# A softplus feed-forward behind decay attention: blocks of 512 tokens in place of 256, and a planner that writes out every engine's order

## The chip, the cores and the metric

The kernel runs on one core of one Trainium2 chip. A core has five engines, each with its own queue of instructions: TensorE (PE in the profile; its weight loads are shown apart as PEld), VectorE (DVE), ScalarE (ACT), GpSimd (POOL) and SyncE (SP), which here only issues DMAs. They work side by side and wait for each other by semaphores. The metric is the device time of one execution in microseconds (us); lower is better.

## The reference

Attention with a decaying state per head, then a feed-forward layer with softplus:

```python
for t in range(S):                      # q, k, v: 4 batches, 8 heads, 768 tokens, 64 wide
    state = gamma[None, :, None, None] * state + np.einsum('bhd,bhe->bhde', k[:, :, t], v[:, :, t])
    y[:, :, t] = scale * np.einsum('bhd,bhde->bhe', q[:, :, t], state)
x = np.ascontiguousarray(y.transpose(0, 2, 1, 3)).reshape(B * S, H * D)      # 3072 tokens x 512
h = x @ w_in                            # 512 x 2048
g = np.maximum(h, 0.0) + np.log1p(np.exp(-np.abs(h)))
return (g @ w_out).astype(np.float32)   # 2048 x 512
```

The weights are float64 in memory; the kernel reads them as pairs of 32-bit words and makes float32 of them.

## The kernel before, in words

**Attention** is cut into 48 units: 4 batches, 6 chunks of 128 tokens, two halves of four heads. Inside a chunk it is matrix work: scores of the chunk (`sc`), masked below the diagonal; the state that the chunk adds (`pp`, kept as `td`); and the outputs (`yp`), scores times values plus queries times the state so far (`st`). A unit begins with transposes of k and q (`tp`), and its outputs go into `xh` and `xl`, the layer's input. The decay is in tables: GpSimd scales q and v (lines 120 and 121). A first chunk of a batch has no state to read, a last one none to make.

**Precision.** The large products are made of float32r matmuls on split operands: a value is a rounded part (`...h`) plus the rest (`...l`), and a product is three matmuls, hh, hl and lh (lines 289 to 291 and 319 to 321). The splitting is work for ScalarE (the rounding copy), VectorE or GpSimd (the subtraction). The first `WHOLE` = 8 units aren't split: their matmuls are float32 (lines 166, 194, 243 and 249), which take two instructions each and fewer on ScalarE and VectorE.

**The feed-forward** takes blocks of T = 256 tokens. A step is a pair of the 16 slices of 128 hidden columns: `hidden` has 24 matmuls of 256 columns into one PSUM bank `hp`; softplus is VectorE (line 296), ScalarE (297), VectorE (301), all in place in `sp`, then ScalarE rounds to `gh` (303) and GpSimd makes `gl` (305); `second` has 12 matmuls of 512 columns (two slices, two token tiles, three products) into the two accumulators of the block. `second` runs `LAG` = 2 steps behind `hidden`. Blocks 0 and 1 are taken in four turns (`TURNS`), since the weights are not all there yet: 0 has three steps, 1 has six, 0 the rest, 1 the rest. A turn that does not end its block leaves its accumulators in SBUF as `part` (line 327), which is added at the end (331).

**The weights** are converted once, slice by slice, in the first part of the run (lines 82 to 95): a scaling by ScalarE, two or three bit operations on VectorE, a rounding by ScalarE, a subtraction by GpSimd, for `win` and `wout` each. Loads run `FETCH` = 3 slices ahead.

**What sets the order.** The source calls the parts of the units by ticks (`PARTS`, `tick`), mixed with the steps; the tile framework then schedules the instructions by its own simulated timeline, and each engine runs its queue in that order. PSUM has eight banks: two `hp`, two accumulators, one for the weights' bits (`wp`), three for attention. `sp`, `gh` and `gl` have two buffers each, k, q and v three.

Of the kernel before, what the change touches and what calls it, by code (L numbers as in the profile page):

```python
# [10 lines left out]
F32 = mybir.dt.float32  # L11
# [6 lines left out]
P = 128  # L18
C = 128
T = 256  # L20
AHEAD = 2
EARLY = 4
WHOLE = 8
TURNS = ((0, 0, 3), (1, 0, 6), (0, 3, 8), (1, 6, 8))
SPREAD = 8
LAG = 2
FETCH = 3
SLACK = 2.0**-17


@with_exitstack
def decay_attention_then_softplus_ffn(ctx: ExitStack, tc: tile.TileContext, q, k, v, w_in, w_out, qtab, vtab, gtab, out):
# [6 lines left out]
    NP = NF // 2  # L39
    HH = H // 2  # L40
    NJ = HH // 2
    NT = T // P

    const = ctx.enter_context(tc.tile_pool(name="const", bufs=1))
    attn = ctx.enter_context(tc.tile_pool(name="attn", bufs=1))
    ffn = ctx.enter_context(tc.tile_pool(name="ffn", bufs=2))
    ps_h = ctx.enter_context(tc.tile_pool(name="ps_h", bufs=2, space=bass.MemoryType.PSUM))
    ps_o = ctx.enter_context(tc.tile_pool(name="ps_o", bufs=1, space=bass.MemoryType.PSUM))
    ps_w = ctx.enter_context(tc.tile_pool(name="ps_w", bufs=1, space=bass.MemoryType.PSUM))
    ps_a = ctx.enter_context(tc.tile_pool(name="ps_a", bufs=3, space=bass.MemoryType.PSUM))  # L50
# [3 lines left out]
    gtab_sb = const.tile([P, 2, H], F32, name="gtab_sb")  # L54
    qtabs = const.tile([P, NC, H], F32, name="qtabs")
    vtabs = const.tile([P, NC, H], F32, name="vtabs")
    ident = const.tile([P, P], F32, name="ident")


    raw, win, wout, converts = {}, {}, {}, {}  # L60

    def load_weights(f):
        fs = slice(f * P, (f + 1) * P)
        raw[f] = [const.tile([P, ND * P], I64, name=nm, tag=f"{nm}{f}") for nm in ("win", "wout")]
        loads_of_f = (
            nc.sync.dma_start(raw[f][0].rearrange("p (c w) -> p c w", c=ND), w_in[:, fs].rearrange("(c p) w -> p c w", p=P)),
            nc.sync.dma_start(raw[f][1], w_out[fs, :]),
        )

        if f >= FETCH:  # L70
            for load, after in zip(loads_of_f, converts[f - FETCH]):
                tc.add_manual_dep(load.ins, after.name, mybir.DependencyInfo(mybir.DependencyClass.Sync, mybir.DependencyReason.SCHED_ONLY), reason="pace")

    def convert_weights(f):

        n = ND * P
        converts[f] = []
        for nm, bits, to in zip(("win", "wout"), raw.pop(f), (win, wout)):
            words = bits.bitcast(U32).rearrange("p (n t) -> p n t", t=2)
            low, high = words[:, :, 0], words[:, :, 1]  # L80

            nc.scalar.activation(high.bitcast(F32), high.bitcast(F32), AF.Copy, scale=2.0**-112)

            wp = ps_w.tile([P, n], U32, name="wp")
            w = ffn.tile([P, n], U32, name="w", tag="o")

            if nm == "wout":
                nc.scalar.activation(wp, low, AF.Copy, scale=(1 - SLACK) * 2.0**-29, bias=7.5 * SLACK - 0.5)
            else:
                nc.vector.tensor_scalar(wp, low, 29, None, op0=ALU.logical_shift_right)  # L90
            nc.vector.scalar_tensor_tensor(wp, high, 0x80000000, wp, op0=ALU.bitwise_and, op1=ALU.bitwise_or)
            nc.vector.scalar_tensor_tensor(w, high, 3, wp, op0=ALU.logical_shift_left, op1=ALU.bitwise_or)
            to[f] = const.tile([P, 2, n], F32R, name=f"{nm}hl", tag=f"{nm}{f}")
            converts[f].append(nc.scalar.copy(to[f][:, 0], w.bitcast(F32)).ins)
            nc.gpsimd.tensor_tensor(to[f][:, 1], w.bitcast(F32), to[f][:, 0].bitcast(F32), op=ALU.subtract)
# [3 lines left out]
    loads, live, state, xs = {}, {}, {}, {}  # L99
    lo, up = slice(0, D), slice(D, P)  # L100


    kqs = [attn.tile([P, 3, 2, NJ, C], F32R, name=f"kq{i}") for i in range(2)]

    qws = [attn.tile([P, 2, NJ, C], F32, name="qw", tag="vhl", bufs=2) for i in range(2)]

    def load_unit(n):
        b, c, hf = units[n]
        tiles = []
        for nm, src in (("kn", k), ("qn", q), ("vn", v)):  # L110
            t = attn.tile([P, HH, D], F32, name=nm, bufs=3)
            nc.sync.dma_start(t, src[b, hf * HH:(hf + 1) * HH, c * C:(c + 1) * C, :].rearrange("h s d -> s h d"))
            tiles.append(t)
        loads[n] = tiles

    def decay(n):
        b, c, hf = units[n]
        kn, qn, vn = loads[n]
        hs = slice(hf * HH, (hf + 1) * HH)
        nc.gpsimd.tensor_tensor(qn, qn, qtabs[:, c, hs].unsqueeze(2).broadcast_to([P, HH, D]), op=ALU.mult)  # L120
        nc.gpsimd.tensor_tensor(vn, vn, vtabs[:, c, hs].unsqueeze(2).broadcast_to([P, HH, D]), op=ALU.mult)

# [324 lines left out]
```

## Time and profile before

| | |
|---|---|
| time, median of 3 runs | 703.34 us (702.11 to 703.37) |
| span of the profiled execution, first to last instruction | 700.0 us |
| its distance to that median, taken as what lies around the span | 3.34 us |
| mean granted clock of TensorE | 0.995 |
| TensorE busy | 682.3 us (97%) |
| VectorE, ScalarE, GpSimd busy | 453.1, 369.2, 284.1 us |
| DMA | 42.83 MB, 61 GB/s in the mean, 266 and 296 GB/s in the first two of 40 slices |

The runs give times alone, so the profiled execution is known by its span. In the page, slices are fortieths of the span (17.5 us). In a row of the timeline stand the start, the duration, engine, line, operation, output and inputs, shape and count, and in brackets how long the engine was idle before and what ended that. A matmul's duration holds its passage through the array and overlaps the next one; what a matmul costs in a row of them is the distance between starts. In a row of the groups stand the total, the mean in ns, and the idle time before.

### The profile page before, as it was taken

How to read it: one execution, taken by the hardware profiler on the slowest of the kernel's cores; microseconds unless marked ns; L12 is line 12 of the kernel's file. 1: busy time of each engine (PE TensorE's matmuls, PEld its weight loads, DVE VectorE, ACT ScalarE, POOL GpSimd, SP SyncE). 2: the span in 40 equal slices, each digit the busy share in tenths (PEclk: the TensorE clock that was granted, in tenths of full speed). 3: DMA queues.
4: the chain of work that ended last, by engine and by line, in shares of the span. 5: the costliest groups of instructions: out<-in, count | busy, mean ns of one | idle time of the engine just before them, and what ended most of it. 6: DMA issues, size and time to landing. Idle time of an engine off the chain costs nothing.

```text
span 700.0 us, 13586 instructions
## 1 busy us (share of the span) xinstructions
PE 682.3 (97%) x5056; PEld 621.6 (89%) x5056; DVE 453.1 (65%) x935; ACT 369.2 (53%) x831; POOL 284.1 (41%) x326
## 2 busy tenths in 40 slices
PE   5898999999999999999999999999999999999997
PEld 4687889999999999999999999999999999999996
DVE  5789979676666666567667766647766676544221
ACT  5888767555455545445555555545455545543221
POOL 6676566543343343344333333433442333222221
PEclk9999899999999999999999999999999999999999
DMA  9967452022112111111111111211211110000000
GB/s 266 296 188 188 120 173 59 16 61 68 32 23 69 24 32 58 36 31 54 39 24 31 53 38 24 61 31 31 62 25 38 54 31 16 31 1 1 31 1 30
DMA packets 90753, 42.83 MB, mean 61 GB/s; under 512 B 77376, under 2 KB 85568, under 8 KB 90688
## 3 DMA queue, kind: packets, MB, share of 16 engines
q1 hardware_dynamic: 90240, 41.96, 22.2%
q8 instruction: 40, 0.66, 0.4%
q14 instruction: 25, 0.20, 0.1%
q10 hardware_dynamic: 448, 0.01, 0.0%
HBM read 35.66 MB, written 6.29 MB: 60 GB/s over the span
## 4 chain that ended last, share of the span: by engine, by line
PE 93%; DVE 2%; ACT 1%; issue 1%; POOL 0%; ACTq 0%; DVEq 0%
PE hp L289 14%; PE hp L290 13%; PE hp L291 13%; PE acc L319 13%; PE acc L320 12%; PE acc L321 12%; PE sc L174 3%; PE pp L198 2%; PE tp L130 1%; PE yp L254 1%; PE yp L253 1%; PE tp L128 1%; PE yp L252 1%; PE yp L246 1%; PE yp L245 1%
## 5 line engine op out<-in xcount | busy, mean ns | idle before, releaser
L289 PE MATMUL hp<-xh,winhl 128*128 128x256 f32 x768 | 221.5, 289 | 1.2 <-DVE sp L301 1.1
L290 PE MATMUL hp<-xl,winhl 128*128 128x256 f32 x768 | 218.8, 285 | 0.0
L291 PE MATMUL hp<-xh,winhl 128*128 128x256 f32 x768 | 218.3, 284 | 0.0
L305 POOL TENSOR_TENSOR gl<-sp,gh 128x512 fp32r<-128x512 f32 x96 | 126.2, 1315 | 145.9 <-ACT gh L303 85.8
L319 PE MATMUL acc<-wouthl,gh 128*128 128x512 f32 x384 | 153.7, 400 | 0.0
L320 PE MATMUL acc<-wouthl,gh 128*128 128x512 f32 x384 | 150.5, 392 | 0.0
L289 PEld LDWEIGHTS hp<-xh,winhl 128*128 128x128 f32 x768 | 147.2, 192 | 3.1 <-issue 1.4
L321 PE MATMUL acc<-wouthl,gl 128*128 128x512 f32 x384 | 149.5, 391 | 0.0
L290 PEld LDWEIGHTS hp<-xl,winhl 128*128 128x128 f32 x768 | 148.0, 193 | 1.6 <-issue 0.3
L291 PEld LDWEIGHTS hp<-xh,winhl 128*128 128x128 f32 x768 | 147.8, 192 | 0.2
L296 DVE TENSOR_SCALAR sp<-hp 128x512 uint32<-128x512 uint32 x96 | 66.2, 690 | 69.7 <-PE hp L291 60.0
L303 ACT CAST gh<-sp 128x512 fp32r<-128x512 f32 x96 | 59.4, 620 | 76.4 <-PE acc L320 56.6
L120 POOL TENSOR_TENSOR qn<-qn,qtabs 128x256 f32<-128x256 f32 x48 | 29.7, 618 | 160.8 <-DMA qn<-in_q_dram 130.3
L297 ACT ACTIVATE sp<-sp 128x512 f32<-128x512 f32 x96 | 60.9, 634 | 53.2 <-DVE sp L296 52.8
L321 PEld LDWEIGHTS acc<-wouthl,gl 128*128 128x128 f32 x384 | 72.0, 188 | 15.7 <-issue 0.2
L319 PEld LDWEIGHTS acc<-wouthl,gh 128*128 128x128 f32 x384 | 72.4, 189 | 12.0
L320 PEld LDWEIGHTS acc<-wouthl,gh 128*128 128x128 f32 x384 | 72.5, 189 | 11.8 <-issue 0.2
L145 DVE TENSOR_TENSOR kq<-tp,kq 64x256 fp32r<-64x256 f32 x80 | 33.8, 422 | 68.9 <-ACT kq L143 67.5
L301 DVE SCALAR_TENSOR_TENSOR sp<-hp,sp 128x512 f32<-128x512 f32 x96 | 65.9, 687 | 13.0 <-ACT sp L297 11.7
L142 ACT CAST kq<-tp 64x512 fp32r<-64x512 f32 x80 | 46.5, 581 | 42.6 <-PE tp L130 41.6
L260 DVE TENSOR_TENSOR xl<-yp,xh 64x256 fp32r<-64x256 f32 x96 | 40.0, 417 | 32.0 <-ACT xh L258 30.9
L258 ACT CAST xh<-yp 64x256 fp32r<-64x256 f32 x96 | 35.1, 366 | 46.0 <-PE yp L254 43.6
(85 smaller groups left out, 1103.8 us busy)
## 6 DMA issues: line engine op xcount, KB each, us to landing
win<-in_moe_w_in_dram SPq DMA_DIRECT2D x16, 512.0 KB, 4.5
wout<-in_moe_w_out_dram SPq DMA_DIRECT2D x16, 512.0 KB, 4.0
kn<-in_k_dram SPq DMA_DIRECT2D x48, 128.0 KB, 2.3
qn<-in_q_dram SPq DMA_DIRECT2D x48, 128.0 KB, 2.8
vn<-in_v_dram SPq DMA_DIRECT2D x48, 128.0 KB, 2.2
out_dram<-o SPq DMA_DIRECT2D x24, 256.0 KB, 2.1
gtab_sb<-in_gtab_dram ACTq DMA_DIRECT2D x2, 2.0 KB, 3.9
qtabs<-in_qtab_dram ACTq DMA_DIRECT2D x1, 4.0 KB, 2.3
```

The source lines that it names most:

```text
L142: nc.scalar.copy(kq[own, :2, par], tp[own])
L289: nc.tensor.matmul(hp[:, k], lhsT=wt[:, 0, d, :], rhs=xh[:, d, :], start=d == 0, stop=False)
L290: nc.tensor.matmul(hp[:, k], lhsT=wt[:, 0, d, :], rhs=xl[:, d, :], start=False, stop=False)
L291: nc.tensor.matmul(hp[:, k], lhsT=wt[:, 1, d, :], rhs=xh[:, d, :], start=False, stop=d == ND - 1)
L296: nc.vector.tensor_scalar(sp.bitcast(U32), hps[s].bitcast(U32), 0x80000000, None, op0=ALU.bitwise_or)
L297: nc.scalar.activation(sp, sp, AF.Softplus)
L301: nc.vector.scalar_tensor_tensor(g, hps.pop(s), 0.0, g, op0=ALU.max, op1=ALU.add)
L303: nc.scalar.copy(gh, g)
L305: nc.gpsimd.tensor_tensor(gl, sps.pop(s), gh.bitcast(F32), op=ALU.subtract)
L319: nc.tensor.matmul(acc[i][t], lhsT=gh[:, k, ts], rhs=wt[:, 0], start=begins and k == 0, stop=False)
L320: nc.tensor.matmul(acc[i][t], lhsT=gh[:, k, ts], rhs=wt[:, 1], start=False, stop=False)
L321: nc.tensor.matmul(acc[i][t], lhsT=gl[:, k, ts], rhs=wt[:, 0], start=False, stop=ends and k == 1)
```

## The change

The file is written anew; the instructions of a unit, of a step and of a weight slice are as before, with these differences:

- **T = 512.** A feed-forward step is now one slice of hidden columns for 512 tokens: 12 matmuls of 512 columns into `hp`, the same chain of softplus, and 12 matmuls into four accumulators, all eight with gh first and then the four with gl (in the last step of a block token tile by token tile). There are 6 blocks of 16 steps. Only in block 0 four steps are made for half a block and two slices at a time, 256 columns wide, as soon as units 0 to 3 or 4 to 7 are there. No `part` is left.
- **WHOLE = 14**: units 8 to 13 are float32 too.
- **Banks and buffers.** Four accumulators, two `hp`, two banks `a0`, `a1` for attention and the weights' bits (early on the accumulators are lent to them). `sp` has one buffer in place of two; k, q and v have two in place of three, and three units at a time borrow the not yet loaded places of the last weights. `FETCH` is 2.
- **A planner.** All instructions are put in a list as operations with a cost, what they come after, the buffers they use and, for some, a due time. `Planner.order` plays that list with its costs and hand-over times, on each engine takes the operation that can start first and among those the one due first, and the instructions are then emitted in that order, each chained to the one before on its engine, so that the framework keeps it. The first three units' loads now stand ahead of the first weights in SP's queue.

The core of the diff:

```diff
-T = 256
-WHOLE = 8
-TURNS = ((0, 0, 3), (1, 0, 6), (0, 3, 8), (1, 6, 8))
-LAG = 2
-FETCH = 3
+T = 512
+W = 256
+WHOLE = 14
+BORROW = 8
+ORDER = ("u0", "u1", "u2", "u3", "u4", "h0", "u5", "h0", "u6", "u7", "h1", "h1")
+FETCH = 2
+HANDOVER = {
+    "PE": {"ACT": 210, "DVE": 250, "POOL": 300, "PE": 0, "SP": 300},
...
+                first = min(c[0] for c in starts)
+                if first >= 1e12 or best is not None and first >= best[0]:
+                    continue
+                s, b, op = min((c for c in starts if c[0] <= first + 1e-6), key=lambda c: (c[1] + COMFORT[e] > c[0], c[2].due, c[2].number))
...
+    hold_sp = holder(pool, [P, T], F32, "sp0")
+    hold_gh = holder(pool, [P, T], F32R, "gh0", "gh1")
+    hold_gl = holder(pool, [P, T], F32R, "gl0", "gl1")
...
-    def hidden(s):
-        i, p = steps[s]
-        xh, xl = xs[i]
-        hp = hps[s] = ps_h.tile([P, 2, T], F32, name="hp")
-        for k in range(2):
-            wt = win[2 * p + k].rearrange("p t (c f) -> p t c f", c=ND)
-            for d in range(ND):
-                nc.tensor.matmul(hp[:, k], lhsT=wt[:, 0, d, :], rhs=xh[:, d, :], start=d == 0, stop=False)
-                nc.tensor.matmul(hp[:, k], lhsT=wt[:, 0, d, :], rhs=xl[:, d, :], start=False, stop=False)
-                nc.tensor.matmul(hp[:, k], lhsT=wt[:, 1, d, :], rhs=xh[:, d, :], start=False, stop=d == ND - 1)
+    def ffn_step(s, h, i, f, when):
+        halves = slice(0, T // W) if h is None else h
+        n = 1 if h is None else T // W
+        width = T // n
...
+                    xh, xl = xt[:, 0, halves, d, :], xt[:, 1, halves, d, :]
+                    mm(o, wt[:, 0, d, :], xh, d == 0, False)
+                    mm(o, wt[:, 0, d, :], xl, False, False)
+                    mm(o, wt[:, 1, d, :], xh, False, d == ND - 1)
...
+        for part in range(1 if ends else 2):
+            for t in ts:
...
+                        if ends or part == 0:
+                            mm(bank(acc), buf(gh)[:, tt], wt[:, 0], begins and k_ == 0, False)
+                            mm(bank(acc), buf(gh)[:, tt], wt[:, 1], False, False)
+                        if ends or part == 1:
+                            mm(bank(acc), buf(gl)[:, tt], wt[:, 0], False, ends and k_ == n - 1)
```

How the order moves, at three places. First TensorE in the middle of the run, from a unit's transposes (`tp` before, L356 after) towards its scores (`sc` from `kq`). Before, the transposes:

```order
L289 MATMUL hp<-xh,winhl 128x256
L290 MATMUL hp<-xl,winhl 128x256
L291 MATMUL hp<-xh,winhl 128x256
L128 MATMUL tp<-ident,kn 128x128 x2
L130 MATMUL tp<-ident,qn 128x128 x2
L319 MATMUL acc_6363<-wouthl,gh 128x512
L320 MATMUL acc_6363<-wouthl,gh 128x512
L321 MATMUL acc_6363<-wouthl,gl 128x512
```

After, all of the way from the last transposes to the scores (`x` is the layer's input, `win` and `wout` the split weights, `a` a bank of attention):

```order
L356 MATMUL a_3767<-ident,qn_3478 128x128 x2
L270 MATMUL hp_3775<-x_68,win_933 128x512 x3
L270 MATMUL acc_3183<-wout_960,gh_3773 128x512 x2
L270 MATMUL acc_3190<-wout_960,gh_3773 128x512 x2
L270 MATMUL acc_3231<-wout_960,gh_3773 128x512 x2
L270 MATMUL acc_3213<-wout_960,gh_3773 128x512 x2
L270 MATMUL acc_3183<-wout_960,gl_3786 128x512
L270 MATMUL acc_3190<-wout_960,gl_3786 128x512
L270 MATMUL acc_3231<-wout_960,gl_3786 128x512
L270 MATMUL acc_3213<-wout_960,gl_3786 128x512
L270 MATMUL hp_3775<-x_68,win_933 128x512 x6
L270 MATMUL a_3813<-kq_67 128x256 x2
```

Hidden matmuls are 512 wide, the second product takes four accumulators, and 21 matmuls stand between a unit's transposes and its scores; before, behind the rows shown, it was a whole `second` (12), the outputs of the unit before (20 of 128 columns) and a whole `hidden` (24).

Second, TensorE near the end of the run. Before, the tail of the second product (`acc0`, `acc1`), where its last step's gh_8510 comes up for the first time:

```order
L319 MATMUL acc1_8288<-wouthl_1399,gh_8465 128x512
L320 MATMUL acc1_8288<-wouthl_1399,gh_8465 128x512
L321 MATMUL acc1_8288<-wouthl_1399,gl_8467 128x512
L319 MATMUL acc0_8287<-wouthl_1514,gh_8510 128x512
L320 MATMUL acc0_8287<-wouthl_1514,gh_8510 128x512
L319 MATMUL acc1_8288<-wouthl_1514,gh_8510 128x512
L320 MATMUL acc1_8288<-wouthl_1514,gh_8510 128x512
L321 MATMUL acc0_8287<-wouthl_1514,gl_8512 128x512
```

After, from the last hidden step to the same place (gh0_7114 and gl0_7118 come from the hidden step ahead, hp1_7050; gh1_7134 and gl1_7136 from the last one, hp0_7097):

```order
L270 MATMUL hp1_7050<-x1_69,win14_1310 128x512 x3
L270 MATMUL hp0_7097<-x1_69,win15_1363 128x512 x12
L270 MATMUL acc0_6639<-wout14_1457,gh0_7114 128x512 x2
L270 MATMUL acc1_6643<-wout14_1457,gh0_7114 128x512 x2
L270 MATMUL acc2_6675<-wout14_1457,gh0_7114 128x512 x2
L270 MATMUL acc3_6663<-wout14_1457,gh0_7114 128x512 x2
L270 MATMUL acc0_6639<-wout14_1457,gl0_7118 128x512
L270 MATMUL acc1_6643<-wout14_1457,gl0_7118 128x512
L270 MATMUL acc2_6675<-wout14_1457,gl0_7118 128x512
L270 MATMUL acc3_6663<-wout14_1457,gl0_7118 128x512
L270 MATMUL acc0_6639<-wout15_1486,gh1_7134 128x512 x2
L270 MATMUL acc0_6639<-wout15_1486,gl1_7136 128x512
```

Before, the last hidden matmul stands 24 matmuls of the second product ahead of the first one that reads gh_8510; after, 12 ahead of the first one that reads gh1_7134, and gl1_7136 is wanted two matmuls later.

Third, ScalarE in the start, at the first units behind the eighth, with weights (`raw`, `win`, `wout`, `w`) and softplus (`sp`, `gh`) around it. Before, unit 9 is split (`kq`, `vhl`, `ah` in two pieces):

```order
L142 CAST kq_82<-tp 64x2x256
L143 CAST kq_82<-tp 64x256
L142 CAST kq_82<-tp 64x2x256
L143 CAST kq_82<-tp 64x256
L82 ACTIVATE wout<-wout 128x512
L297 ACTIVATE sp<-sp 128x512
L149 CAST vhl<-vn 128x4x64
L94 CAST winhl<-w 128x512
L88 ACTIVATE wp<-wout 128x512
L303 CAST gh<-sp 128x512 x2
L176 CAST ah<-sc 128x256 x2
```

After, unit 8 is float32 (`kh` and `qw` are plain copies of the transposes):

```order
L473 CAST x_69<-a_1086 64x2x128
L372 COPY kh_1118<-a_1040 128x256
L374 COPY qw_73<-a_1040 64x256
L294 ACTIVATE raw<-raw 128x512
L473 CAST x_69<-a_1086 64x2x128
L294 ACTIVATE raw<-raw 128x512
L298 ACTIVATE a_1145<-raw 128x512
L317 CAST win_1152<-w_1143 128x512
L540 ACTIVATE sp_1150<-sp_1150 128x512
L317 CAST wout_1174<-w_1168 128x512
```

The four casts to `kq` and the one to `vhl` are gone; in their place stand two copies.

More of the change, by code (lines that the diff above doesn't have):

```diff
@@ new lines, with __init__ @@
+class Op:
+    def __init__(self, engine, cost, run, after, uses, at):
+        if engine in ("ACT", "DVE", "POOL"):
+            cost *= SLOW
+        self.engine, self.cost, self.run, self.uses, self.at = engine, cost, run, uses, at
+        self.after, self.then, self.start, self.end = [], [], None, None
+        for a in after:
+            if a is not None and a not in self.after:
+                self.after.append(a)
+                a.then.append(self)
+        for u in uses:
+            u.users.append(self)
@@ L31, in decay_attention_then_softplus_ffn @@
+MARGIN = 0
+SLOW = 1.02
+SHARED = ("hp0", "hp1", "acc0", "acc1", "acc2", "acc3", "a0", "a1")
+COMFORT = {"PE": 0, "ACT": 100, "DVE": 100, "POOL": 100, "SP": 0}
 @with_exitstack
@@ L52, in decay_attention_then_softplus_ffn @@
-    nc.scalar.preload_act_table_set("softplus")
[L54 to L72, printed above, removed]
+    NB = B * S // T
@@ new lines, in decay_attention_then_softplus_ffn, with hl, PE, ACT @@
+    weights = {}
+    LATE = [f"{nm}{f}" for f in (NF - 1, NF - 2) for nm in ("win", "wout")]
+    def hl(nm, f):
+        if (nm, f) not in weights:
+            weights[nm, f] = pool.tile([P, 2, ND * P], F32R, name=f"{nm}{f}")
+        return weights[nm, f]
+    bank = buf
+    def PE(n, run, after, uses=(), at=None):
+        return plan.add("PE", n, run, after, uses, at)
+    def ACT(n, run, after, uses=(), at=None):
+        return plan.add("ACT", n, run, after, uses, at)
+    def DVE(n, run, after, uses=(), at=None):
+        return plan.add("DVE", n, run, after, uses, at)
@@ L74, in convert_weights, with POOL, DMA @@
+    def POOL(n, run, after, uses=(), at=None):
+        return plan.add("POOL", n, run, after, uses, at)
+    def DMA(size, run, after=(), uses=(), at=None):
+        return plan.add("SP", size / 316.0, run, after, uses, at)
+    mm = lambda o, l, r, start, stop: emit(nc.tensor.matmul(o, lhsT=l, rhs=r, start=start, stop=stop))
+    wdone, pace = {}, []
     def convert_weights(f):
         n = ND * P
[L77 to L85, printed above, removed]
-            if nm == "wout":
-                nc.scalar.activation(wp, low, AF.Copy, scale=(1 - SLACK) * 2.0**-29, bias=7.5 * SLACK - 0.5)
-            else:
[L90 to L95, printed above, removed]
@@ L411, in decay_attention_then_softplus_ffn @@
-    for s, (i, p) in enumerate(steps):
-        convert_to(2 * p + 2)
-        stages(s, plan[s])
-        convert_to(EARLY + s + 1)
-    for s in range(len(steps), len(steps) + LAG):
-        stages(s, done)
+        for t in ts:
+            acc, done = accs.pop((i, t))
+            ob = hold_w(queue=False)
+            if t % 2:
+                o = ACT(scalar_time(DM), lambda acc=acc, ob=ob: emit(nc.scalar.copy(buf(ob), bank(acc))), [done[-1]], [acc, ob], when[1] + 3000)
+            else:
+                o = DVE(vector_time(DM), lambda acc=acc, ob=ob: emit(nc.vector.tensor_copy(buf(ob), bank(acc))), [done[-1]], [acc, ob], when[1] + 3000)
+            r = slice(i * T + t * P, i * T + (t + 1) * P)
+            DMA(4 * P * DM, lambda r=r, ob=ob: emit(nc.sync.dma_start(out[r, :], buf(ob))), [o], [ob], when[1] + 3000)
@@ L420 @@
+    ordered = plan.order()
+    for op in ordered:
+        op.run()
 def kernel(**inputs):
```

714 lines of the change are left out of this document (446 added, 268 removed).

## The prediction

> **What bounds the kernel now.** I read the page first: the busy shares, the slices, and the engines of the chain that ended last.
>
> ```profile
> span 700.0 us, 13586 instructions
> PE 682.3 (97%) x5056; PEld 621.6 (89%) x5056; DVE 453.1 (65%) x935; ACT 369.2 (53%) x831; POOL 284.1 (41%) x326
> PE   5898999999999999999999999999999999999997
> PE 93%; DVE 2%; ACT 1%; issue 1%; POOL 0%; ACTq 0%; DVEq 0%
> ```
>
> TensorE (PE) is the bound: 93% of the chain, and full from the fifth slice to the last but one. Only slices 1 to 5 (the first 88 us) and the last one hold idle time. But "busy" overlaps (ends are modelled), so a full digit does not say how much work is in it. For that I take the groups by form and then the timeline of one steady stretch, where the distance from one start to the next is the price of a matmul.
>
> ```profile
> L289 PE MATMUL hp<-xh,winhl 128*128 128x256 f32 x768 | 221.5, 289 | 1.2 <-DVE sp L301 1.1
> L319 PE MATMUL acc<-wouthl,gh 128*128 128x512 f32 x384 | 153.7, 400 | 0.0
> L166 PE MATMUL sc<-qw,kw 128*128 128x128 f32 x64 | 11.4, 312 | 2.5 <-ACT qw L135 1.7 <-DVE qw L136 0.7
> ```
> ```profile
> 500.86 0.22 PE L252 MATMUL yp<-ah,vhl 128*64 128x128 f32 x1
> ...
> 501.58 0.33 PE L289 MATMUL hp<-xh,winhl 128*128 128x256 f32 x1
> 501.75 0.28 PE L290 MATMUL hp<-xl,winhl 128*128 128x256 f32 x1
> ...
> 504.50 0.64 PE L174 MATMUL sc<-kq 128*128 128x256 f32 x4
> 504.99 0.40 PE L319 MATMUL acc<-wouthl,gh 128*128 128x512 f32 x1
> 505.22 0.40 PE L320 MATMUL acc<-wouthl,gh 128*128 128x512 f32 x1
> ...
> 507.73 0.22 PE L198 MATMUL pp<-vhl,kh 128*64 128x128 f32 x1
> ...
> 508.17 0.36 PE L289 MATMUL hp<-xh,winhl 128*128 128x256 f32 x1
> 508.37 0.28 PE L290 MATMUL hp<-xl,winhl 128*128 128x256 f32 x1
> ...
> 694.21 0.39 PE L319 MATMUL acc<-wouthl,gh 128*128 128x512 f32 x1
> ...
> 695.34 0.39 PE L321 MATMUL acc<-wouthl,gl 128*128 128x512 f32 x1
> ```
>
> From 501.75 to 504.50 stand the other 23 matmuls of a hidden step, 256 columns each: 0.1196 us apiece. From 505.22 to 507.73 stand 11 of 512 columns: 0.228; in the tail, from 694.21 to 695.34, five: 0.226; I take 0.227. A float32r unit costs 0.49 for its scores (504.50 to 504.99), 0.44 for its states (507.73 to 508.17) and 0.06 for each output matmul (12 of them from 500.86 to 501.58). The first hidden matmul behind a piece of attention takes 0.17 or 0.20 in place of 0.12 (501.58 and 508.17): taking 0.09 behind the transposes too, some 0.22 a unit, and the change keeps these seams.
>
> Now the whole: 2304 x 0.1196 = 276 (three lines of 768), 1152 x 0.227 = 262, 40 float32r units 93 (0.36 for the transposes of each included, by pairs like the one at 511.34 below), 8 float32 units 28 (their prices below): 658 us of matmuls in a span of 700. Of the other 42, 4.4 lie behind the last matmul, 48 x 0.22 = 10.6 are seams, and 27 are lost in the first 90 us. So the change can gain by fewer us of matmul, or by a faster start.
>
> **The change, term by term.** The sum is made against the span, 700.0, and its own 3.34 us up to the median of the three runs (703.34) are kept.
>
> *Wider hidden matmuls.* Before, 2304 of 256 columns; after, the order holds 1104 of 512 and 96 of 256 (the four half-block steps). A pair of 256 costs 0.239, one of 512 costs 0.227: 1104 x 0.012 = **-13.2**, all on PE's path. From the two prices a matmul has 0.012 us that do not depend on its columns. The Trainium skill ("TensorE: Matmul & The Clock Gate", section "Back-to-back issue gap") puts the gap between warm matmuls at N / 2.4 + 2.5 ns, hence 0.0025 us of fixed cost; by that, an estimate from that page, the term would be 1104 x 0.0025 = -2.8 and the sum below 702.1. The trace does not agree: 0.1196 stands where the page would have 0.109. I go by the rows.
>
> *Six more units in float32* (8 to 13). Their price from the early units:
>
> ```profile
> 56.40 0.38 PE L243 MATMUL yp<-qw,st 128*64 128x128 f32 x2
> ...
> 57.49 0.38 PE L249 MATMUL yp<-ah,vn 128*64 128x128 f32 x2
> ...
> 59.06 0.83 PE L166 MATMUL sc<-qw,kw 128*128 128x128 f32 x6
> 59.82 0.68 PE L194 MATMUL pp<-vn,kn 128*64 128x64 f32 x8
> 60.42 0.72 PE L321 MATMUL acc<-wouthl,gl 128*128 128x512 f32 x2
> ```
>
> Outputs: 10 matmuls from 56.40 to 57.49, 0.109 each; scores 0.127 each (six in 0.76), eight a unit (64 for 8 units); states 0.60. Against a float32r unit: scores 1.02 for 0.49, states 0.60 for 0.44, outputs 16 x 0.109 = 1.74 for 20 x 0.06 = 1.20 (in a first chunk, without state, 0.87 for 0.72). Units 8 and 9 cost 1.23 more each, 10 and 11 (a last chunk, no states) 1.07, 12 and 13 (a first chunk) 0.84: **+6.3** on PE.
>
> *The start.* What the six units buy: ScalarE issues 7 instructions for a float32 unit against 13, VectorE 4 against 16.
>
> ```profile
> 6.00:20.00 14.00, 10.60 (x65) 8.20 (x66) 11.63 (x29) 10.91 (x26) 7.40 (x9) 1.00 1.16 316
> 20.00:60.00 40.00, 38.38 (x284) 32.03 (x284) 32.78 (x58) 33.58 (x75) 29.18 (x33) 1.00 0.83 229
> ...
> 66.00:68.00 2.00, 0.64 (x6) 0.40 (x4) 1.82 (x4) 1.93 (x5) 0.61 (x1) 1.00 0.68 231
> ...
> 70.00:72.00 2.00, 1.40 (x11) 1.13 (x11) 1.92 (x5) 1.32 (x3) 0.43 (x1) 0.50 0.85 266
> ```
>
> The columns are PE, weight loads, VectorE, ScalarE, GpSimd, granted clock. At 66 to 68 PE works 0.64 of 2 us while VectorE and ScalarE are over 90% full with the conversions of weights and the first split units; then the clock is at 0.50. The new order has less of that work at this place, and none of it is new. How much of the 27 goes? The latest thing in the new start is ScalarE: ahead of gh_825 (softplus of the third step, first half-block of the second pair) stand 16 + 6 + 13 instructions on weights, 9 copies of 512, 36 of 256, 16 of 128 and 6 of the softplus.
>
> ```profile
> L82 ACT ACTIVATE win<-win 128x512 f32<-128x512 f32 x16 | 11.0, 685 | 3.1 <-DMA win<-in_moe_w_in_dram 2.9
> L94 ACT CAST winhl<-w 128x512 fp32r<-128x512 f32 x16 | 9.9, 619 | 3.3 <-DVE w L92 3.2
> L167 ACT COPY ah<-sc 128x512 f32<-128x512 f32 x8 | 4.7, 581 | 0.5 <-PE sc L166 0.4
> L258 ACT CAST xh<-yp 64x256 fp32r<-64x256 f32 x96 | 35.1, 366 | 46.0 <-PE yp L254 43.6 <-PE yp L249 1.3
> L217 ACT COPY st<-td 64x128 f32<-64x128 f32 x6 | 1.8, 295 | 0.1
> ```
>
> 16 x 0.685 + 25 x 0.619 + 9 x 0.581 + 36 x 0.366 + 16 x 0.295 = 49.6 us. PE has 47.9 us of matmuls ahead of the same place (40 transposes 3.5, 72 scores 9.1, 64 states 4.8, 112 outputs 12.2, 96 hidden of 256 columns 11.5, 30 of 512 6.8), and some 2 of seams. If ScalarE starts at 6 us and is as full as before between 6 and 60 (44.5 of 54, 82%), gh_825 comes at 66.5, so 16.6 us are lost by then, and about 1 more behind it, since ScalarE's next 12 us of work (at 90%, 13.3) stand against 12.2 of PE: 17.7 lost in place of 27, a gain of 9. At 95% full it comes at 58.2 and the gain is 17. If the waits only move, it is 0. I take **-9**, by the fullness that the row shows.
>
> *The end.* Before, 24 matmuls of the second product stand between the last hidden matmul and the first one that reads its gh; after, 12, with one sp buffer in place of two. The chain behind a hidden step:
>
> ```profile
> 687.26 0.28 PE L291 MATMUL hp<-xh,winhl 128*128 128x256 f32 x1
> ...
> 687.65 0.69 DVE L296 TENSOR_SCALAR sp<-hp 128x512 uint32<-128x512 uint32 x1 [3.54 <-PE hp L291]
> ...
> 689.04 0.69 DVE L301 SCALAR_TENSOR_TENSOR sp<-hp,sp 128x512 f32<-128x512 f32 x1 [0.70 <-ACT sp L297]
> 690.10 0.62 ACT L303 CAST gh<-sp 128x512 fp32r<-128x512 f32 x1 [1.09 <-PE acc L320]
> ...
> 690.85 1.29 POOL L305 TENSOR_TENSOR gl<-sp,gh 128x512 fp32r<-128x512 f32 x1 [4.33 <-ACT gh L303]
> ```
>
> The hidden step ends at 687.38 (0.12 behind 687.26), and VectorE begins 0.27 later. The cast could have begun at 689.76, when VectorE was done; it waited 0.34 for its buffer, which is free in the new order. Without that wait gh is there 3.05 and gl 4.45 us behind the hidden step's end. In the new order the last hidden step ends 2.72 (12 x 0.227) behind the one ahead of it, and its sp has to wait for that step's gl: VectorE begins 1.75 behind its end in place of 0.27, so its gh is there at 4.55 and its gl at 5.95. PE waits 0.35 for the gh of the step ahead, works 2.72 to 3.05, waits 1.5 for the last gh, does two matmuls and waits 0.95 for the last gl: **+2.8**.
>
> *In between.* A unit's scores wait for the chain from its transposes:
>
> ```profile
> 511.34 0.38 PE L130 MATMUL tp<-ident,qn 128*128 128x128 f32 x2
> ...
> 515.06 0.43 DVE L146 TENSOR_TENSOR kq<-tp,kq 64x256 fp32r<-64x256 f32 x1
> ...
> 518.45 0.64 PE L174 MATMUL sc<-kq 128*128 128x256 f32 x4
> ```
>
> From the end of the transposes (0.14 behind 511.34) to the last kq (515.49) are 4.0 us, and PE had 7.0 us of other work there (to 518.45). In the new order it has between 4.3 and 5.3 in most units (the place in the order shown above: 21 matmuls of 512, 4.8). That fits with 0.3 to 1.3 to spare; a softplus instruction that gets into it makes a small wait. Bounds 0 and 23 (below); I take **+1.5**, nearer the row that fits.
>
> The evictions of partial sums (4, by VectorE and ScalarE) go; those engines have slack from slice 6 on, so 0. With GpSimd, seams and the last output copies nothing changes.
>
> Sum: -13.2 + 6.3 - 9 + 2.8 + 1.5 = -11.6. Span 688.4, time **691.7**.
>
> **The rivals.**
>
> The start does not get better: its waits move to ScalarE's copies of the first units, which have to go through before any weights are converted (three units' loads now stand ahead of the first weights on SP's queue). For it: ScalarE is on PE's heels by my own sum. Against: the clock drop at 70 came from a stall of split units that are gone. Time: 691.7 + 9 = 700.7.
>
> Width saves nothing: a hidden matmul of 512 columns costs what two of 256 cost, 0.239, since it is its weight load or its moving operand that sets the pace. For it: no row shows a hidden matmul of that width. Against: the second product has weights of the same 128 x 128 and 512 columns, and costs 0.227. Without the 13.2 the time is 704.9, which is at the edge of what can be told (+0.2%). The page named above lies between, at 702.1 by the estimate there.
>
> The fixed order makes waits in every unit: one VectorE instruction of the softplus (0.69 in the row above) gets into each of the 34 float32r chains of 4.0 us. PE takes its instructions in order, so each such wait is lost: 34 x 0.69 = 23.5 in place of 1.5, time 713.7. It is slower from a mean wait of 0.39 us a unit on ((11.6 + 1.5) / 34). For it: 4.3 is little more than 4.0. Against: before, ScalarE and VectorE are idle a third of a steady stretch, and any us that PE loses at seams gives them room.
>
> That the change doesn't do what it says can be left out: the order shows 512 columns and 14 float32 units.
>
> **How the numbers follow.** Forecast 0.66, no better start 0.18, no gain by width 0.04 (counted as same), waits in every unit 0.12. A measurement of this kernel can tell about 0.2% (1.4 us) from no change. Faster: forecast and worse start, 0.84. Same: 0.04. Slower: 0.12. Low end: start at 17 and no waits, 691.7 - 8 - 1.5 = 682, taken as 683; high end 702, which takes in the case of no better start and the upper bounds of the start in the forecast. Outside lie the waits in every unit (0.12), no gain by width (0.04) and the forecast's far edges.
>
> **What would show it.** Right: hidden matmuls start 0.227 apart; the slices show PE full from about 60 us, no slice with the clock down after 20; the last 10 us show PE idle for some 3 us, waiting for GpSimd's gl. Wrong: scores or outputs that wait on VectorE or GpSimd by 10 us in all; a hidden matmul at 0.239; PE not full before 85 us.

## The result, and the profile after

The changed kernel takes 692.93 us in the median of four runs (691.09 to 695.19), the kernel before 702.73 in four runs beside them: a ratio of 0.9863, 95% interval 0.9835 to 0.9891. Forecast were 691.7 us. The profiled execution took 691.09 us with a span of 689.4, 10.6 less than the span before.

The page, in the lines that answer to those of before:

```profile
span 689.4 us, 11100 instructions
PE 671.6 (97%) x3952; PEld 561.8 (82%) x3952; DVE 413.3 (60%) x867; ACT 358.7 (52%) x799; POOL 276.8 (40%) x320
PE   6998999999999999999999999999999999999995
PEclk9999999999999999999999999999999999999999
```

TensorE is at 8 or 9 from the second slice to the last but one, and in this execution the clock stays up, where before it fell at 70 us. Two windows of the start (columns as before: PE, weight loads, VectorE, ScalarE, GpSimd, granted clock):

```profile
20.00:60.00 40.00, 38.02 (x300) 33.94 (x299) 30.09 (x55) 31.74 (x71) 27.82 (x33) 1.00 0.73 211
60.00:82.00 22.00, 20.41 (x103) 16.56 (x101) 19.25 (x32) 17.43 (x32) 15.10 (x13) 1.00 0.50 171
```

ScalarE is 79% full between 20 and 60 us, where it was 84%, and 22 us around the old stall miss 1.6 us of TensorE's work.

The timeline of TensorE in a steady stretch gives the price of the new matmul:

```profile
305.28 1.52 PE L270 MATMUL hp<-x,win 128*128 128x512 f32 x6
306.64 0.64 PE L270 MATMUL a<-kq 128*128 128x256 f32 x4
307.12 2.91 PE L270 MATMUL hp<-x,win 128*128 128x512 f32 x12
309.86 0.22 PE L270 MATMUL a<-vhl,kh 128*64 128x128 f32 x1
```

Six hidden matmuls of 512 columns take 1.36 us (305.28 to 306.64), 0.227 each; twelve take 2.74, 0.228 each. The main waits of TensorE in the whole run, from the list of waits (sum, number, longest):

```profile
PE a L356 <- POOL qn L348: 4.7, 1, 4.7
PE hp L270 <- DVE sp L541: 1.6, 1, 1.6
PE acc L270 <- ACT gh L542: 1.4, 2, 1.2
PE hp L270 <- DVE x L474: 1.0, 1, 1.0
...
PE acc L270 <- POOL gl L543: 0.7, 1, 0.7
PE a L270 <- DVE td L485: 0.6, 1, 0.6
```

The first stands ahead of the first matmul of all, those on sp and x in the first 65 us, those on gh and gl in the last fourteen. Only the 0.6 on td (at 293 us) lies in the steady part. The end, from the timeline:

```profile
675.82 1.30 POOL L543 TENSOR_TENSOR gl<-sp,gh 128x512 fp32r<-128x512 f32 x1 [5.34 <-ACT gh L542]
677.15 0.69 DVE L539 TENSOR_SCALAR sp<-hp 128x512 uint32<-128x512 uint32 x1 [2.17 <-POOL gl L543]
...
679.99 0.73 PE L270 MATMUL acc<-wout,gh 128*128 128x512 f32 x2 [1.21 <-ACT gh L542]
...
681.40 0.50 PE L270 MATMUL acc<-wout,gl 128*128 128x512 f32 x1 [0.67 <-POOL gl L543]
...
683.57 0.39 PE L270 MATMUL acc<-wout,gl 128*128 128x512 f32 x1
684.83 0.59 ACT L576 COPY w<-acc 128x512 f32<-128x512 f32 x1 [1.61 <-DMA out_dram<-w]
685.54 0.69 DVE L578 COPY w<-acc 128x512 f32<-128x512 f32 x1 [2.91 <-ACT w L576]
```

VectorE cannot begin the last softplus before GpSimd has read the one sp buffer (677.15), and TensorE waits 1.21 and 0.67 for what comes of it. Behind the last matmul (683.57, its end 0.23 later) the third and fourth output copies wait for the stores of the first two, since there are two w buffers for four outputs: 5.6 us from the last matmul to the end of the span, 4.4 before.

### The profile page after: what moved, and what is told of

It is laid out like the page before. It is cut to its first block, busy times and chain, and to the rows that moved or that the text cites. A ratio compares the mean times of both kernels' runs of the same rounds, so it can differ in the third digit from the quotient of the medians.

```text
span 689.4 us, 11100 instructions
## 1 busy us (share of the span) xinstructions
PE 671.6 (97%) x3952; PEld 561.8 (82%) x3952; DVE 413.3 (60%) x867; ACT 358.7 (52%) x799; POOL 276.8 (40%) x320
## 3 DMA queue, kind: packets, MB, share of 16 engines
q1 hardware_dynamic: 90240, 41.96, 22.2%
## 5 line engine op out<-in xcount | busy, mean ns | idle before, releaser
L270 PE MATMUL hp<-x,win 128*128 128x512 f32 (+1 forms) x1200 | 297.7, 388 | 2.6 <-DVE sp L541 1.6
L270 PEld LDWEIGHTS hp<-x,win 128*128 128x128 f32 x1200 | 213.4, 188 | 42.8 <-issue 2.9
L270 PE MATMUL acc<-wout,gh 128*128 128x512 f32 x768 | 202.3, 395 | 1.4 <-ACT gh L542 1.4
L270 PEld LDWEIGHTS acc<-wout,gh 128*128 128x128 f32 x768 | 139.4, 188 | 29.7 <-ACT gh L542 2.3
L270 PE MATMUL acc<-wout,gl 128*128 128x512 f32 x384 | 108.8, 391 | 0.7 <-POOL gl L543 0.7
L270 PEld LDWEIGHTS acc<-wout,gl 128*128 128x128 f32 x384 | 71.2, 188 | 15.7 <-POOL gl L543 1.1
L412 ACT CAST kq<-a 64x512 fp32r<-64x512 f32 x68 | 39.5, 581 | 22.9 <-PE a L356 17.2
L348 POOL TENSOR_TENSOR qn<-qn,qtabs 128x256 f32<-128x256 f32 x46 | 28.5, 620 | 47.3 <-DMA qn<-in_q_dram 42.6
L270 PE MATMUL a<-ah,vhl 128*64 128x128 f32 x272 | 40.8, 222 | 0.0
L474 DVE TENSOR_TENSOR x<-a,x 64x256 fp32r<-64x256 f32 x86 | 35.8, 416 | 8.4 <-ACT x L473 7.1
L270 PE MATMUL a<-kq,st 128*64 128x128 f32 x240 | 34.1, 223 | 0.0
```

The lines of the kernel that those rows point to most:

```text
L270: mm = lambda o, l, r, start, stop: emit(nc.tensor.matmul(o, lhsT=l, rhs=r, start=start, stop=stop))
L348: scaled = lambda t, tab: emit(nc.gpsimd.tensor_tensor(t, t, tab[:, c, hs].unsqueeze(2).broadcast_to([P, HH, D]), op=ALU.mult))
L412: ck.append(ACT(scalar_time(512), lambda par=par, own=own: emit(nc.scalar.copy(KQ[int(kq.slot[-1])][own, par, :2], tpv()[own])), [tk, tq], ...
L474: xl.append(DVE(vector_time(256), lambda par=par, r=r: emit(nc.vector.tensor_tensor(xo(1, r), ypv()[:, par], xo(0, r).bitcast(F32), op=ALU ...
```

## The experiments

Theories: the terms of the prediction's sum, each with the reason given there, against the rivals named with each experiment. The last column is the median against that of the changed kernel in the first row. Not all of the kernels ran on the same chip, but each had the kernel before beside it (medians 702.24 to 702.98); taken from the ratios, the last column moves by 0.6 us at most. With intervals of about 0.15% on each side, differences below 1.5 us can't be told by time alone, and are read from rows. An edit of the changed kernel also goes through the planner, which may answer it with another order.

| kernel | median us | ratio to the kernel before, interval | against the changed kernel |
|---|---|---|---|
| the changed kernel again | 691.99 | 0.9849 [0.9834, 0.9864] | |
| hidden matmuls of 256 columns | 705.98 | 1.0042 [1.0028, 1.0056] | +14.0 |
| WHOLE = 8 | 730.23 | 1.0379 [1.0351, 1.0406] | +38.2 |
| WHOLE = 12 | 692.14 | 0.9850 [0.9834, 0.9865] | +0.2 |
| the kernel before with WHOLE = 14 | 702.09 | 0.9996 [0.9986, 1.0005] | |
| ScalarE: six bits instructions twice | 695.23 | 0.9897 [0.9877, 0.9917] | +3.2 |
| two sp buffers in the last block | 695.85 | 0.9905 [0.9891, 0.9918] | +3.9 |
| own sp for the last step | 692.17 | 0.9844 [0.9826, 0.9863] | +0.2 |
| four output buffers | 692.25 | 0.9857 [0.9839, 0.9875] | +0.3 |
| work ahead of the first load | 691.14 | 0.9839 [0.9824, 0.9853] | -0.9 |
| the three edges together | 688.89 | 0.9806 [0.9789, 0.9824] | -3.1 |
| the edges, bits on VectorE | 688.04 | 0.9795 [0.9779, 0.9810] | -4.0 |

### The width

```diff
+                    if h is None:
+                        z = d // NJ
+                        o = bank(hp).rearrange("p (a w) -> p a w", w=W)[:, z]
+                        for c in (2 * d % ND, 2 * d % ND + 1):
+                            mm(o, wt[:, 0, c, :], xt[:, 0, z, c, :], c == 0, False)
...
+                        return
```

> The 92 full hidden steps made of matmuls of 256 columns (24 a step) in place of 512 (12), all else as in the changed kernel. Theory: a pair costs 0.239 against 0.227, 1104 pairs, so +13.2 us against the changed kernel (about 705). Rival 1, the rule of the Trainium skill (TensorE: Matmul & The Clock Gate, Back-to-back issue gap), a fixed cost of 2.5 ns: +2.8 us (about 695). Rival 2: width costs nothing, 0 us (692).

Measured +14.0 us. In this kernel's timeline 24 hidden matmuls of 256 columns stand in a row:

```profile
311.71 3.04 PE L270 MATMUL hp<-x,win 128*128 128x256 f32 x24
314.59 0.22 PE L270 MATMUL a<-vhl,kh 128*64 128x128 f32 x1
```

2.88 us, 0.120 each, 0.240 a pair against 0.227. The order is otherwise that of the changed kernel, but for a stretch at about 160 to 180 us; between 100 and 200 us TensorE waits 0.9 us in all, where the changed kernel does not wait. By the rows 1104 pairs cost 13 to 14 us more. So the width alone is worth what the prediction took, and the two rivals (+2.8 and 0) fall.

### What the six float32 units buy

```diff
-WHOLE = 14
+WHOLE = 8
```

> Units 8 to 13 split again (WHOLE = 8), all else as in the changed kernel. Theory: TensorE has 6.3 us less of matmuls, but the start loses again what it lost before (27 us against 19.4 after), so +7.6 - 6.3 = +1.3 us against the changed kernel (-2 to +4), with ScalarE over 80% full from 20 to 60 us and gh of the third step later than 62.6 us. Rival 1: the fixed order alone mended the start, and the six units are a loss: -6.3 us. Rival 2: split units make more of the latency chain than before since k, q and v have two buffers: +10 us and more.

Measured +38.2 us. Only rival 2 has the size, and it is right about the latency chain; its reason, two buffers for k, q and v, does not show: no wait of TensorE between 100 and 200 us is for their loads. Rival 1 is right about the start, which is not worse: TensorE is busy 20.58 of 22 us between 60 and 82 us here, 20.41 in the changed kernel. The loss is later. Three windows of this kernel, one of the changed kernel, and this kernel's two largest waits between 100 and 200 us:

```profile
60.00:82.00 22.00, 20.58 (x101) 16.73 (x100) 19.17 (x35) 15.39 (x28) 14.60 (x13) 1.00 0.47 156
130.00:148.00 18.00, 13.87 (x68) 11.17 (x67) 12.53 (x23) 10.10 (x21) 7.81 (x9) 0.81 0.16 45
148.00:190.00 42.00, 22.39 (x154) 18.56 (x153) 27.79 (x68) 20.70 (x55) 9.77 (x16) 0.62 0.22 57
```
```profile
148.00:190.00 42.00, 42.00 (x263) 34.73 (x262) 31.74 (x69) 23.82 (x56) 17.15 (x21) 1.00 0.20 54
```
```profile
PE a L270 <- DVE al L446: 11.9, 9, 2.2
PE a L270 <- DVE x L474: 5.2, 3, 2.4
```

and the timeline of TensorE at that place:

```profile
148.13 0.39 PE L270 MATMUL acc<-wout,gl 128*128 128x512 f32 x1
...
152.07 0.47 PE L270 MATMUL a<-kq 128*128 128x256 f32 x2 [2.35 <-DVE x L474]
154.14 0.47 PE L270 MATMUL a<-kq 128*128 128x256 f32 x2 [1.60 <-DVE al L446]
...
190.67 1.63 PE L270 MATMUL hp<-x,win 128*128 128x512 f32 x3
```

At 148.13 the last matmul of block 0's feed-forward is done, and the next feed-forward matmul starts at 190.67: block 1 needs the units 8 to 15, and they aren't there. In between TensorE has only attention, and sits through the chain of every unit (al, x, td, kq). No other engine is full: VectorE works 27.79 of 42 us, ScalarE 20.70. With the gaps the clock falls to 0.62, so that the matmuls that are there take longer too. In the changed kernel the same 42 us are full at clock 1.00. So the float32 units, whose chain is short, don't relieve the start: they let eight units get done while block 0 still has feed-forward work to cover them. The scores that wait for al or x in the rows above read neither of them (their input is kq): they wait for the attention bank that they will write. There are two such banks, where the kernel before had three; what a third would have saved here was not tried.

How near the edge is this cover?

```diff
-WHOLE = 14
+WHOLE = 12
```

> WHOLE = 12: units 12 and 13 split, 8 to 11 float32. Theory: the float32 units buy that block 0's feed-forward steps cover the chain of the units that block 1 needs; with four of six the cover is short by the last units only, so -1.7 us of matmuls and +2 to +10 us of waits between 130 and 190 us (WHOLE = 8 lost 33 us there). Rival 1: the cover is enough with four, -1.7 us. Rival 2: any split unit among these brings the clock down and most of the loss, +20 us or more.

Measured +0.2 us. The list of waits has one of 1.4 (transposes on x) and one of 0.2 (on al) between 100 and 200 us, and the changed kernel has none there: 1.6 us lost for 1.7 of matmuls saved. That is a little below the 2 to 10 us of waits that the theory gave, and rival 1 (-1.7) can't be told from it by time. At twelve the first waits show; the other 38 us lie between twelve and eight, where nothing was run.

The same question in the old order:

```diff
-WHOLE = 8
+WHOLE = 14
```

> The kernel before with WHOLE = 14 and nothing else changed. The prediction's reason: units 8 to 13 in split form are what stalls TensorE between 60 and 80 us; in float32 some 5 us of the 27 lost at the start come back and the matmuls cost 6.3 more, so +1.3 us against the kernel before (-1 to +3), and the slices at 60 to 80 us are full. Rival 1: the start does not depend on these units, +6.3 us. Rival 2: as in the changed kernel with WHOLE = 8, the split units cost far more than they save also in the old order, so -5 us or more.

Measured 702.09 against 702.43 for the kernel before: no difference that can be told. What the six units cost in matmuls (6.3 us, as worked out) comes back. Between 64 and 72 us, where before PE was idle a third of the time and the clock fell, all is full:

```profile
64.00:68.00 4.00, 4.00 (x35) 3.58 (x35) 2.71 (x5) 2.85 (x8) 2.34 (x3) 1.00 0.64 177
68.00:72.00 4.00, 4.00 (x37) 3.93 (x37) 3.88 (x8) 3.16 (x7) 2.53 (x4) 1.00 0.90 236
```

So the prediction's reason holds for the old order, where units 8 and 9 stood in the start among the conversions of weights. In the new order TensorE loses no more there with WHOLE = 8 than with 14, as the 20.58 of 22 us above show.

### Is ScalarE the pace of the start?

```diff
+                if f < 6:
+                    b = ACT(
...
+                        [b], [wp, raw],
+                    )
```

> For the first six weight slices ScalarE makes the bits of wout twice (six more instructions of 0.63 us, 3.8 us of ScalarE's time, ahead of the third step's gh). The prediction's theory: ScalarE sets the pace of the start at some 80% full, so its gh comes 3.8 to 4.8 us later and the time rises by as much. Rival: the start is set by the chains between engines, and ScalarE's gaps take the extra work in: 0 to +1 us.

Measured +3.2 us, near the theory by size. By place it fits less well: gh of the third step begins at 63.53 against 62.56 in the changed kernel, 1.0 later and not 3.8. TensorE works 36.20 us between 20 and 60 in place of 38.02; the rest is small waits on several engines. The planner also answers the six instructions with another order from about 27 us on: the ninth gh starts at 99.76 against 102.52 in the changed kernel, the 26th at 231.84 against 229.39. So the 3.2 us are not lost at one place, and the run does not tell ScalarE's pace from the price of the other order. From the other side, on top of the kernel with the three edges (below):

```diff
-            if nm == "wout":
+            if nm == "none":
                 b = ACT(
```

> The kernel with the three edits at the edges, and the bits of wout made by VectorE as those of win are: ScalarE has sixteen instructions of 0.63 us less, six of them ahead of the third step's gh, VectorE sixteen of 0.69 more. Theory (six more of these on ScalarE cost about 3 us): six fewer bring back about as much, -2 to -3.5 us against the kernel with the edges alone (688.9), so about 686. Rival: VectorE is as full as ScalarE between 20 and 60 us (30 of 40), so the work only changes engines: -0.5 to +2.

Measured 688.04 against 688.89: -0.9, between theory and rival, and the intervals overlap. The window of 20 to 60 us of this kernel:

```profile
20.00:60.00 40.00, 37.33 (x293) 33.21 (x291) 36.83 (x68) 30.22 (x67) 29.07 (x33) 1.00 0.73 218
```

VectorE is 92% full in place of 76% (30.26 of 40 without this edit), and PE works 37.33 us there, 38.21 in the kernel without this edit. That speaks for a pace that ScalarE does not set alone, and for VectorE as the next limit. It is argued, not shown, since here too the order is another one, from about 20 us on.

### The spread, and the slow first matmuls

> The changed kernel unaltered, so that the variants beside it have it on the same chip. Theory: 691 to 694 us, ratio to the kernel before 0.983 to 0.990, with runs that spread by about 4 us where those of the kernel before spread by 1.5. Rival: the spread of the first runs was chance and closes to 1.5 us.

691.99 us, 690.53 to 693.58. The runs spread by 3.1 us, but in nine runs the kernel before has nearly the same, 2.7: nothing shows that the changed kernel spreads more, but the spread itself stays. Two profiles of the same order (the changed kernel, and the one with four output buffers, whose order differs in its last lines alone) show one source. The changed kernel, then the other (the `f32 x6` and `f32 x8` rows are scores of the first units):

```profile
8.16 0.94 PE L270 MATMUL acc<-qw,kh 128*128 128x128 f32 x6 [0.15 <-DVE qw L375]
...
10.53 1.16 PE L270 MATMUL a<-qw,kh 128*128 128x128 f32 x8 [0.24 <-ACT kh L372]
```
```profile
8.02 1.65 PE L270 MATMUL acc<-qw,kh 128*128 128x128 f32 x6 [0.19 <-DVE qw L375]
...
11.80 1.95 PE L270 MATMUL a<-qw,kh 128*128 128x128 f32 x8
```

The same eight scores take 1.95 us in place of 1.16. In one execution the array gets fast at about 8 us, in the other at about 13.4, though the granted clock of the windows reads 1.00 in both. The lead lasts: the 26th gh starts at 229.4 in the one and 231.4 in the other. The Trainium skill ("TensorE: Matmul & The Clock Gate", section "What's actually happening") says that the array starts throttled and is released after a window of about 3.4 us of sustained work, and that the window runs free of the kernel. The traces agree that the array starts slow; they don't agree with the 500 ns by which the moment varies there, since it varies by some 5 us between executions of one order.

A second source shows in the profile of the run just above, the changed kernel again. Its array gets fast at about 8 us too, and yet its 26th gh starts at 231.28. It waits 2.46 us for a softplus where the first profile waits 1.59:

```profile
63.21 2.90 PE L270 MATMUL hp<-x,win 128*128 128x512 f32 x6 [2.46 <-DVE sp L541]
```

The granted clock reads 0.50 from 64 to 66 us, and these six matmuls take 2.70 us (63.21 to 65.91); in the first profile they take 1.47 (62.67 to 64.14), at clock 1.00.

The next kernel goes for the first source:

```diff
+    warm = pool.tile([P, 64], F32, name="warm")
+    emit(nc.vector.memset(warm, 0.0))
+    hot = psum.tile([P, 512], F32, name="hp0")
+    for _ in range(12):
+        mm(hot[:64, :64], warm, warm, True, True)
```

> Twelve float32 matmuls of 64 columns on a zeroed tile stand ahead of TensorE's first transposes, where it waits for the first load anyway; their result is used by nothing. In the profiles the first matmuls take twice as long until 8.5 us in one run and until 13.3 in another, with the same order of instructions. Theory: the array starts slow and gets fast after a few us of work; with the work moved ahead that slow stretch falls into the idle time, so -2 to -4 us against the changed kernel, and a smaller spread. Rival: the first units wait for their loads and for ScalarE, so the time is unchanged (0 to -0.5).

Measured -0.9 us, which can't be told, with a spread of 1.5 (690.79 to 692.27): the spread as expected, the gain smaller. The timeline shows that the array gets fast no earlier:

```profile
1.06 2.82 PE L270 MATMUL hp<-warm 128*64 128x64 f32 x24 [1.06 <-DVE warm L609]
4.59 0.66 PE L356 MATMUL a<-ident,kn 128*128 128x128 f32 x2 [0.71 <-DMA kn<-in_k_dram]
...
7.22 1.55 PE L270 MATMUL acc<-qw,kh 128*128 128x128 f32 x8
8.70 0.68 PE L270 MATMUL acc<-vn,kn 128*64 128x64 f32 x8
```

The extra work ends at 3.88, then TensorE is idle for 0.71, and the array still gets fast only at about 8. With fifteen such matmuls and no gap (the kernel with the three edits, below) it is fast at the first transposes:

```profile
1.06 3.38 PE L270 MATMUL hp<-warm 128*64 128x64 f32 x30 [1.06 <-DVE warm L610]
4.37 0.44 PE L356 MATMUL a<-ident,kn 128*128 128x128 f32 x2
```

0.44 for the transposes in place of 0.66. That the gap decided is not shown, and another profile speaks against it: in the kernel that also makes the bits on VectorE the same fifteen matmuls stand without a gap, the transposes still take 0.66, and the array gets fast at about 6.3:

```profile
4.54 0.66 PE L356 MATMUL a<-ident,kn 128*128 128x128 f32 x2
```

### The end

```diff
+        ... hold_sp(("sp0", "ah0")) if i == NB - 1 else hold_sp() ...
```

> In the last block the softplus buffer alternates between sp0 and a free attention tile, so VectorE need not wait for GpSimd's gl of the step ahead. Theory: TensorE's waits in the tail fall from about 3.3 us (1.4 + 0.7 + 1.2) to about 1.7, so -1.6 us; VectorE begins 0.3 us behind the last hidden matmul in place of 1.7. Rival: GpSimd, which makes both gl one behind the other, sets the end anyway: -0.5 us or less.

Measured +3.9 us: slower, where both expected faster or nothing. With a second buffer in all of the last block the planner makes two hidden steps one behind the other, and nine matmuls of the sixteenth stand at the end, behind the second product of the fifteenth, with nothing to cover their softplus:

```profile
678.50 2.20 PE L270 MATMUL hp<-x,win 128*128 128x512 f32 x9
...
683.65 1.22 PE L270 MATMUL acc<-wout,gh 128*128 128x512 f32 x2 [2.95 <-ACT gh L542]
...
685.64 1.05 PE L270 MATMUL acc<-wout,gh 128*128 128x512 f32 x2
686.50 0.63 PE L270 MATMUL acc<-wout,gl 128*128 128x512 f32 x1
```

One wait of 2.95 in place of 1.2 and 0.2, and behind it matmuls of 0.43 (two from 685.64 to 686.50) in place of 0.23, with a granted clock of 0.50 from 684 to 690 us. The buffer was free; the order that the planner made of it was not. So only the last step gets one:

```diff
+        sp = hold_sp(("ah0",), queue=False) if (i, f) == (NB - 1, NF - 1) else hold_sp()
```

> Only the very last step of the feed-forward has a softplus buffer of its own; the order of TensorE's instructions stays as in the changed kernel. Theory: VectorE begins 0.3 us behind the last hidden matmul in place of 1.7; TensorE's wait for the last gh falls from 1.2 us to below 0.3 and that for the last gl stays at 0.7 or falls, so -1.0 to -1.4 us, and nothing slows down behind the wait. Rival: GpSimd makes the two gl one behind the other (1.3 us each) and the last gl comes no earlier: 0 to -0.3.

Measured +0.2 us, which can't be told from nothing; this profile's array got fast late, at about 13.8. Its end is as expected:

```profile
678.91 0.69 DVE L540 TENSOR_SCALAR ah<-hp 128x512 uint32<-128x512 uint32 x1 [0.57 <-PE hp L270]
...
681.96 0.61 PE L270 MATMUL acc<-wout,gh 128*128 128x512 f32 x2
683.17 0.50 PE L270 MATMUL acc<-wout,gl 128*128 128x512 f32 x1 [0.59 <-POOL gl L544]
```

The wait of 1.2 for the last gh is gone, that for the last gl stays. And the stores:

```diff
-            ob = hold_w(queue=False)
+            ob = hold_w(("w0", "w1", "al0", "vhl0")[t:t + 1], queue=False) if i == NB - 1 else hold_w(queue=False)
```

> The last four output copies have four buffers in place of two, so the third and fourth need not wait for the first two stores. Theory: the span ends 4.4 us behind the last matmul as in the kernel before, in place of 5.6: -1.2 us. Rival: the stores queue one behind the other anyway and the last store sets the end: 0.

Measured +0.3 us, again below what can be told; in the profile the span ends 4.4 us behind the last matmul, as expected, in place of 5.6. The three edits together:

> The three edits at the edges together: fifteen idle-time matmuls on a zeroed tile up to the first transposes, a softplus buffer of its own for the very last step, four buffers for the last four output copies. Theory: the single effects add up, -0.9 (early fast array in every run) -1.2 (last gh) -1.2 (last stores) = -3.3 us against the changed kernel, about 688.7, with a spread below 2 us. If the array also gets fast earlier, since no gap is left ahead of the first transposes, another -1 to -2. Rival: the edges hide each other (the last store follows the last copy whatever the tail), 691.

Measured 688.89 us, -3.1, with a spread of 1.9 us and an interval (0.9789 to 0.9824) clear of the changed kernel's. The sum of the expected effects was -3.3; the three medians alone (-0.9, +0.2, +0.3) don't add up to it. The profiles show where the 3.1 us come from. From the gh of the last step but one to the end of the span the changed kernel takes 14.3 us, four buffers make it 13.2, the own sp 12.7, both together 11.2. So the end alone gives the 3.1 us against the quick profile of the changed kernel, and the early matmuls nothing: that gh starts at 675.20 here and at 675.07 there. What they may do is keep late starts away. In the two profiles with them (same order) that gh starts at 675.12 and 675.20, in the four without at 675.07, 676.89, 677.05 and 678.44. With the bits on VectorE as well it is 688.04, the best kernel here: 0.9795 of the kernel before, interval 0.9779 to 0.9810.

## Why the prediction was right, and which of its reasons were not

**The width** was forecast at -13.2, and giving it back costs 14.0. The rows for 256 and 512 columns of the same weights held for a form that no row had shown. The estimate from the 2.5 ns of the Trainium skill ("TensorE: Matmul & The Clock Gate", section "Back-to-back issue gap") falls here: +2.8 would have been measured, not +14.0. That section gives the formula for a matmul taken by itself, without the weight load that each has here.

**The six float32 units** cost 6.3 us of matmuls by the prediction's rows, which no run measured apart: the old order pays what they cost and gets just as much back.

**The start** was forecast at -9. What is left of the -10.6 when the other terms are taken off is -7.6; the size was near. The reason failed: "What the six units buy" was put down to the start, and in the new order they buy nothing there. With WHOLE = 8 the start is as good (20.58 of 22 us at 60 to 82). It is the new order that mended it, whichever of its parts: that was not taken apart. What the units do buy, the cover of block 0, was in no term of the sum; without it the change would have been a loss of 28 us (730.23 against 702.25). The forecast of the third step's gh, 66.5 us, was late (62.56): consecutive instructions of ScalarE overlap (one of 0.68 us starts at 34.85, the next at 35.42), so its work up to there was less than the sum of their durations, 44.15 us in place of 49.6, in 56.56 us, 78% full where 82% were taken:

```profile
6.00:62.56 56.56, 51.71 (x404) 45.40 (x404) 41.56 (x86) 44.15 (x101) 34.93 (x44) 1.00 0.84 238
```

That -7.6 is a remainder. An estimate from TensorE's rows comes nearer to the start itself: count every matmul of a trace at the price that it has in undisturbed rows (0.227 us for 512 columns, 0.1196 for 256, 0.109 to 0.112 for a float32 one of 128, 0.06 for most float32r ones of 128, and so on), and take the sum from the time that has passed. At 90 us TensorE is then 28.5 us behind in the kernel before and 18.4 in the changed one; it is 18.1 in the new order with WHOLE = 8 and 22.2 in the old one with 14. So the start gained some 10 us, and the six units had no part in it. Between 90 and 200 us, where the float32 units stand, the changed kernel loses 3 us more than the kernel before, which no term of the sum had; by the same prices the six units cost 5.0 us and not 6.3.

**The end** was forecast at +2.8 and came at +2.1 (1.4 and 0.7), by the mechanism described. But "with GpSimd, seams and the last output copies nothing changes" failed for the copies: four outputs on two buffers, +1.2.

**In between** +1.5 were taken and 0.6 came. The rival with waits in all 34 chains did not happen; WHOLE = 8 shows that these waits are real as soon as nothing covers them.

**The surroundings of the span** were taken as 3.34 and are 1.7 (691.09 less 689.4): the profiled execution of before was a quicker one than the median, by about 1.6. That mistake made the forecast late by as much, and the missed output copies made it early. That the time comes out within 1.2 us is so in part luck. Spans compare: 688.4 forecast, 689.4 measured, from -13.2 + 6.3 - 7.6 + 2.1 + 1.2 + 0.6 = -10.6.

## What to carry to other kernels

When a change moves work in a fixed order, ask of every slow chain what covers it at its new place, and how much cover is left there: the same six units are worth nothing in one order and 38 us in the other. A planner can turn a freed resource into another order, so a buffer is best given to the one operation that waits for it. And where run-to-run spread hides an effect of 1 us, find what spreads (here, in part, the first 14 us and a wait at 62 us) and take that away first.

## What the runs showed of the hardware

TensorE's first matmuls take about 1.7 times as long (1.95 against 1.16 us for eight scores) until about 8 to 14 us into the run, and the granted clock of the profile reads 1.00 there. With fifteen matmuls on zeros ahead and no gap behind them the array was fast from 4.4 us on in one profile and from about 6.3 in another; with twelve and a gap of 0.71 us, from about 8.

Later in the run waits are followed by a half clock in some executions, and there the profile does show it. A wait of 2.46 us at 62 us was followed by matmuls of 0.45 in place of 0.23 and a clock of 0.50 from 64 to 66 us, one of 1.59 at the same place in another execution was not. Near the end a wait of 2.95 us was followed by matmuls of 0.43, and in the second profile of the changed kernel the waits of 1.2 and 0.7 were enough (clock 0.50 from 684 to 686 us):

```profile
684.55 1.05 PE L270 MATMUL acc<-wout,gh 128*128 128x512 f32 x2
685.40 0.63 PE L270 MATMUL acc<-wout,gl 128*128 128x512 f32 x1
```

while in the first profile the same matmuls took 0.23 behind the same waits. What decides between the two is open.
